# Two of three passes of a split-precision expert layer: weights instead of tokens held in TensorE for the second layers, sums kept transposed

## The chip, the cores and the metric

One NeuronCore of one Trainium2 chip. Times are device microseconds of one execution of the whole program.

## The reference

```
attn = softmax(mask(scale * q @ k^T)) @ v        # 4 x 8 heads, 576 tokens, window 32, half the heads dilated by 4
x    = attn as [2304 tokens, 512]
P    = exp(x @ w_gate - max); 8 rounds of row and column normalisation      # [2304, 8], the shares
for e in 0..7:  out += P[:, e] * (relu(x @ w1[e]) @ w2[e])                  # 512 -> 1024 -> 512
y    = activation(out @ w_in) @ w_out                                       # 512 -> 2048 -> 512, weights in float64
```

## The kernel before

The hidden dimension is cut into units of 512: two for each of the eight experts (16), and four for the last layer pair (called ffn in the code). The 2304 tokens are cut into three passes `k` of 768, each pass into two halves of 384 (`HALF`). Every product is made in split precision: an operand is kept as a high and a low float32r word, and `product` (L413) issues three matmuls for each 128-deep piece: high by high, high by low, low by high. The high word is a copy on ScalarE (L110), the low word a subtraction on VectorE (L111); in the text these are "highs" and "lows".

Unit 0 of all tokens is computed in six blocks of 384 tokens (`block_steps`), mixed by hand with the attention. The blocks of passes 1 and 2 (the last four) send their result to DRAM (`y_kept`). Then the list `runs` is worked off. Pass 0 is done unit by unit (units 1 to 15). Each of the passes 1 and 2 begins with unit 1 alone and goes on with seven pairs: both units of one expert. The ffn ends the program with two pairs for each pass.

A unit's `first_layer` makes 7 products of quarters (a Strassen scheme; `ORDER` is 1, 5, 6, 2, 7, 3, 4) of 12 matmuls each with 384 moving columns: 84 matmuls, in PSUM tiles `pa`, `pb`, `pc`, evacuated by ScalarE and VectorE into `kept`. Its `second_layer` holds 128 tokens in the array and streams 512 columns of the weights `w2o`: 6 token tiles by 4 pieces by 3, 72 matmuls into `py`, and VectorE adds each finished tile to the sum `acc` (tokens by model dimension), scaled by the token's share in `prob`, which is a per-partition scalar there.

A pair does two first layers (`F1`, `F2` below) and then `seven_second`: again 7 products of quarters, here of 256 columns of the weights: for each product 3 token tiles by 4 pieces by 3 matmuls, 252 in all, into `qh` or `qy`, `qt`, `qs` and `qx`. The operands for one product stand in one of three buffers `hh`, `hl`, `third`, written by highs and lows (class `Seven`) as the strings in `FIRST_WORK` and `SECOND_WORK` place them. A low is issued one product or more ahead of its use. After each token tile, VectorE's `join_scaled` (L578) adds the tile to `acc`, times its share.

After each pass `turn_steps` transposes `acc` on TensorE (24 transposes through `ident`, L1186), copies it to `xf` on ScalarE and sends it to `z_kept`, the ffn's input; then `y_kept` of the next pass is loaded into `acc`. All this lies within the first layer that follows.

Beside this runs `double_steps`: it converts the ffn's float64 weights on VectorE (L298 to L335), makes sums on GpSimd (L137, L264), splits and stores them. It is advanced a step at a time (`pull(double)`) at places counted in TensorE's order, in passes 1 and 2. All DMAs are issued by SP's queue, in program order. Engines run their own instructions strictly in order.

## Time and profile before

| | us |
|---|---|
| median of 3 runs | 1971.32 (1970.05 to 1971.91) |
| the profiled execution | 1969.49, of which the span 1967.7 |
| PE busy in the span | 1947.1 (99%) |
| DVE, ACT, POOL busy | 1475.8, 1011.0, 315.9 |
| granted TensorE clock | 1.00 of 2.4 GHz all through |

PE, DVE, ACT, POOL and SP are TensorE, VectorE, ScalarE, GpSimd and SyncE. The busy time of PE is the union of overlapping matmuls, so the time that a matmul costs is read from a stretch divided by its matmuls, not from the duration of one.

### The profile page before, as it was taken

How to read it: one execution, taken by the hardware profiler on the slowest of the kernel's cores; microseconds unless marked ns; L12 is line 12 of the kernel's file. 1: busy time of each engine (PE TensorE's matmuls, PEld its weight loads, DVE VectorE, ACT ScalarE, POOL GpSimd, SP SyncE). 2: the span in 40 equal slices, each digit the busy share in tenths (PEclk: the TensorE clock that was granted, in tenths of full speed). 3: DMA queues.
4: the chain of work that ended last, by engine and by line, in shares of the span. 5: the costliest groups of instructions: out<-in, count | busy, mean ns of one | idle time of the engine just before them, and what ended most of it. 6: DMA issues, size and time to landing. Idle time of an engine off the chain costs nothing.

```text
span 1967.7 us, 34404 instructions
## 1 busy us (share of the span) xinstructions
PE 1947.1 (99%) x12926; PEld 1864.6 (95%) x12926; DVE 1475.8 (75%) x2612; ACT 1011.0 (51%) x2179; POOL 315.9 (16%) x327
## 2 busy tenths in 40 slices
PE   8999999999999999999999999999999999999999
PEld 7888889899898989999999999999999999999999
DVE  6654698988888868686888668677987576876867
ACT  6655445455555445444445435443454355675555
POOL 4213133534544400001001000010011000000000
PEclk9999999999999999999999999999999999999999
DMA  7532577788787888898889977988898877787874
GB/s 167 125 73 85 199 270 278 300 313 311 290 326 299 333 339 305 296 325 324 294 317 328 320 269 279 344 287 314 296 330 320 286 248 283 257 293 269 288 242 145
DMA packets 222390, 539.41 MB, mean 274 GB/s; under 512 B 81040, under 2 KB 113296, under 8 KB 199824
## 3 DMA queue, kind: packets, MB, share of 16 engines
q1 hardware_dynamic: 222224, 537.21, 77.5%
q8 instruction: 102, 1.67, 0.3%
q14 instruction: 64, 0.52, 0.1%
HBM read 383.53 MB, written 153.62 MB: 273 GB/s over the span
## 4 chain that ended last, share of the span: by engine, by line
PE 93%; ACT 2%; DMA 2%; DVE 2%; issue 0%; POOL 0%; SPq 0%; ACTq 0%; POOLq 0%; DVEq 0%
PE pa L413 22%; PE py L413 17%; PE pc L413 11%; PE qy L413 9%; PE qh L413 9%; PE qt L413 9%; PE pb L413 5%; PE qs L413 3%; PE ph L413 3%; PE s L766 2%; PE qx L413 1%; DMA w_kept<-raw 1%; PE px L808 1%; PE pe L792 1%; PE pt L734 1%
## 5 line engine op out<-in xcount | busy, mean ns | idle before, releaser
L413 PE MATMUL pa<-xo,w1o 128*128 128x384 f32 x2736 | 513.7, 336 | 5.9 <-ACT kept L428 4.7
L413 PEld LDWEIGHTS pa<-xo,w1o 128*128 128x128 f32 x2736 | 476.1, 188 | 10.8 <-ACT kept L428 6.7
L413 PE MATMUL pc<-xo,w1o 128*128 128x384 f32 x1368 | 257.2, 335 | 0.8 <-DVE w1o L111 0.8
L137 POOL TENSOR_TENSOR raw<-raw 128x256 f32<-128x256 f32 x152 | 141.2, 957 | 704.5 <-DVE raw L325 170.7
L413 PE MATMUL py<-w2o,hh 128*128 128x512 f32 x816 | 251.5, 390 | 0.0
L413 PEld LDWEIGHTS pc<-xo,w1o 128*128 128x128 f32 x1368 | 238.5, 188 | 1.1 <-DVE w1o L111 1.1
L428 ACT ACTIVATE kept<-pa 128x384 f32<-128x384 f32 x228 | 110.0, 490 | 230.0 <-PE pa L413 228.1
L413 PEld LDWEIGHTS py<-w2o,hh 128*128 128x128 f32 x816 | 152.8, 188 | 30.2
L386 DVE TENSOR_TENSOR xf<-xf 128x768 f32<-128x768 f32 x180 | 167.3, 964 | 1.4
L413 PE MATMUL py<-w2o,hl 128*128 128x512 f32 x408 | 158.8, 389 | 0.0
L110 ACT ACTIVATE third<-xf 128x768 fp32r<-128x768 f32 (+1 forms) x124 | 95.2, 793 | 80.3 <-DVE xf L386 33.1
L111 DVE TENSOR_TENSOR w1o<-raw,w1o 128x256 fp32r<-128x256 f32 x210 | 125.0, 644 | 11.9 <-ACT w1o L110 11.9
L111 DVE TENSOR_TENSOR third<-xf,third 128x768 fp32r<-128x768 f32 (+1 forms) x124 | 115.5, 943 | 19.9 <-ACT third L110 17.9
L413 PE MATMUL pb<-xo,w1o 128*128 128x384 f32 x684 | 129.0, 335 | 0.0
L431 DVE TENSOR_TENSOR kept<-pb,kept 128x384 f32<-128x384 f32 x114 | 62.1, 554 | 84.6 <-PE pb L413 83.9
L1157 ACT ACTIVATE xf<-kept 128x384 f32<-128x384 f32 x168 | 86.2, 524 | 71.1 <-DVE kept L431 69.5
L413 PEld LDWEIGHTS pb<-xo,w1o 128*128 128x128 f32 x684 | 119.1, 188 | 0.0
L110 ACT ACTIVATE w1o<-raw 128x256 fp32r<-128x256 f32 x210 | 77.3, 414 | 70.1 <-POOL raw L137 70.1
L110 ACT ACTIVATE hh<-xf 128x768 fp32r<-128x768 f32 x92 | 74.7, 842 | 70.8 <-DVE xf L386 33.4
L110 ACT ACTIVATE hl<-xf 128x768 fp32r<-128x768 f32 x92 | 74.5, 842 | 63.1 <-DVE xf L386 25.8
L603 ACT ACTIVATE hh<-kept 128x384 fp32r<-128x384 f32 x102 | 53.7, 526 | 80.3 <-DVE kept L431 80.2
L111 DVE TENSOR_TENSOR hh<-xf,hh 128x768 fp32r<-128x768 f32 x92 | 86.8, 957 | 9.3 <-ACT hh L110 9.2
(191 smaller groups left out, 3543.7 us busy)
## 6 DMA issues: line engine op xcount, KB each, us to landing
w1o<-w_kept SPq DMA_DIRECT2D x294, 512.0 KB, 5.7
w2o<-w_sums SPq DMA_DIRECT2D x56, 1024.0 KB, 5.2
w_kept<-w1o SPq DMA_DIRECT2D x105, 512.0 KB, 4.2
w2o<-w_kept SPq DMA_DIRECT2D x40, 1024.0 KB, 5.3
w2x<-w_kept SPq DMA_DIRECT2D x24, 1024.0 KB, 5.7
w2x<-w_sums SPq DMA_DIRECT2D x24, 1024.0 KB, 5.6
w_kept<-w2o SPq DMA_DIRECT2D x23, 1024.0 KB, 6.4
w_kept<-raw SPq DMA_DIRECT2D x36, 512.0 KB, 7.2
```

Source lines behind the costliest of these rows:

```text
L110: nc.scalar.activation(out=hi, in_=raw, func=AF.Copy)
L111: return lambda: nc.vector.tensor_tensor(out=lo, in0=raw, in1=hi.bitcast(F32), op=ALU.subtract)
L137: nc.gpsimd.tensor_tensor(out=out[:, q], in0=in0[:, q], in1=in1[:, q], op=op)
L386: nc.vector.tensor_tensor(out=dst, in0=in0, in1=in1, op=ALU.subtract)
L413: nc.tensor.matmul(o, lhsT=a(h), rhs=b(l), start=first and n == 0, stop=last and n == 2, skip_group_check=on)
L428: nc.scalar.activation(out=dst, in_=src, func=AF.Copy)
L431: nc.vector.tensor_tensor(out=dst, in0=src, in1=dst, op=ALU.add)
L603: return [lambda: nc.scalar.activation(out=hi, in_=src, func=AF.Relu), lambda: nc.vector.scalar_tensor_tensor(out=lo, in0=src, scalar=0.0, ...
L734: nc.tensor.transpose(pt[:, pr, i * CH:(i + 1) * CH], raw[:, 2 * t + i, 2 * pr:2 * pr + 2, :].rearrange("p h e -> p (h e)"), ident[:CH, :CH])
L766: nc.tensor.matmul(s[:, i, :], lhsT=qd[:, pr, j, :], rhs=kt[:, pr, key0(j):key0(j) + KW], start=not early, stop=not early or i == JG - 1)
L792: nc.tensor.transpose(pt[:, i * P:(i + 1) * P], self.e[:, i, :], ident)
L1157: return [lambda: nc.scalar.activation(out=hid[:, half_, j, f], in_=src, func=AF.Relu)]
```

## The change

In passes 1 and 2 the sum `acc` is kept as model dimension by tokens (`acc_t`, the same tile read as 128 x 4 x 768). The second layers of unit 1, of the pairs and of the last four blocks of unit 0 now hold 128 x 128 of the weights in the array and stream 384 tokens. A token's share is now a column, so it can no longer be a per-partition scalar: `shares_steps` transposes `prob` once for each pass and stores it (`p_kept`), `load_shares` loads one expert's row, repeated over all partitions. A finished tile of a pair is multiplied by it on VectorE into a `kept` buffer (`scaled`) and added to `acc_t` on GpSimd. In unit 1, VectorE adds and GpSimd multiplies. `turn_steps` transposes only after pass 0; later it sends `acc_t` out as it is.

```diff
+    acc_t = acc.rearrange("p t d -> p (t d)").rearrange("p (c x) -> p c x", c=KC)
...
+    SECOND_TURNED = ([(f, c, 0) for f in (0, 2) for c in range(3)] + [(f, c, 1) for f in (1, 3) for c in range(3)]
+                     + [(f, c, 1) for f in (0, 2) for c in range(3)] + [(f, c, 0) for f in (1, 3) for c in range(3)]
+                     + [(f, 3, j) for j in range(2) for f in range(FC)])
+
+    def second_layer_turned(finish):
...
+            product(py[c, j], lambda h: w2o[:, h, f, c * P:(c + 1) * P],
+                    lambda h: hs[h][:, f, j * HALF:(j + 1) * HALF], left[c, j] == KC - 1, left[c, j] == 0)
+            if not left[c, j]:
+                finish(py[c, j], c, j)
+            yield "y"
...
+    def seven_second_turned(buf, tag):
...
+            for x in range(2):
+                o = chain[of][x]
+                for c in range(KC):
+                    product(o, lambda h: w[:, h, c, x * P:(x + 1) * P], lambda h: a[:, h, c, :],
+                            of == i and c == 0, c == KC - 1, of != i)
+                    if c == KC - 1:
+                        there = acc_t[:, d * 2 + x, j * HALF:(j + 1) * HALF]
+                        room = late.tile([P, HALF], F32, tag=f"kept{(2 - count) % 3}", bufs=2, name="scaled")
+                        count += 1
+                        nc.vector.tensor_tensor(out=room, in0=o, in1=at.shares[j], op=ALU.mult)
+                        nc.gpsimd.tensor_tensor(out=there, in0=room, in1=there, op=ALU.add)
+                    m = x * KC + c
+                    if m in (2, 5, 7):
+                        yield n, (2, 5, 7).index(m)
...
+        for f, c in [(f, c) for c0 in (0, 2) for f in range(FC) for c in (c0, c0 + 1)]:
...
+            product(py[c], lambda h: at.w2[f][:, h, cs], lambda h: hid[h][:, f, :HALF], f == 0, f == FC - 1)
+            if f == FC - 1:
+                here = at.stage()[:, :HALF]
+                nc.scalar.activation(out=here, in_=py[c], func=AF.Copy)
+                nc.sync.dma_start(out=y_kept[b // 2][:, c, b % 2 * HALF:(b % 2 + 1) * HALF], in_=here)
...
-    def join_scaled(e, k):
-
-        def join(o, i, x, d):
-            at_ = acc[:, x, d * HD:(d + 1) * HD]
-            nc.vector.scalar_tensor_tensor(out=at_, in0=o, scalar=prob[:, k * TPP + x, e:e + 1], in1=at_,
-                                           op0=ALU.mult, op1=ALU.add)
-        return join
+    def load_shares(e, k):
+
+        at.shares = [late.tile([P, HALF], F32, tag="r", bufs=2, name="shares") for _ in range(2)]
+        for j, x in enumerate(at.shares):
+            nc.sync.dma_start(out=x, in_=p_kept[k][e, j * HALF:(j + 1) * HALF].partition_broadcast(P))
+
+    def finish_turned(py, c, j):
+        o = acc_t[:, c, j * HALF:(j + 1) * HALF]
+        nc.vector.tensor_tensor(out=o, in0=py, in1=o, op=ALU.add)
+        nc.gpsimd.tensor_tensor(out=o, in0=o, in1=at.shares[j], op=ALU.mult)
...
-            share = {1: 33 / 48, 2: 60 / 48, 3: 26 / 48}
+            share = {1: 33 / 48, 2: 63 / 48, 3: 28 / 48}
...
+        def turn_steps(k, more):
+
+            if k:
+                yield
+                nc.sync.dma_start(out=z_kept[k].rearrange("p (c x) -> p c x", c=KC), in_=acc_t)
+                for _ in range(9):
+                    yield
+                if more:
+                    nc.sync.dma_start(out=acc_t, in_=y_kept[k + 1])
+            else:
...
-                    if m > 12 or u > 1 and m % 5:
+                    if m > 12 and (u > 1 or m % 3) or u > 1 and m % 5:
                         pull(double)
...
-                if e == 1 and m >= len(ORDER) * UQ - TPP:
-                    t = m - (len(ORDER) * UQ - TPP)
-                    nc.scalar.activation(out=acc[:, t, :], in_=acc[:, t, :], func=AF.Copy,
-                                         scale=prob[:, k * TPP + t, 0:1])
+                if moe and m == 4:
+                    load_shares(e, k)
...
-            for n_, t in seven_second((join_scaled if moe else join_plain)(e, k), bufs, tags[0]):
+            for n_, t in seven_second_turned(bufs, tags[0]) if moe else seven_second(join_plain(e, k), bufs, tags[0]):
```

Over the whole program TensorE has 3528 fewer matmuls of 256 columns (14 pairs by 252), 288 fewer of 512, 48 fewer transposes of 128, and 2736 more of 384 columns. VectorE has 294 fewer joins of 128x256 and 12 fewer of 128x512, and 212 more operations of 128x384 that read PSUM; GpSimd has 212 more of 128x384; SP issues 38 more DMAs.

TensorE, second layers of the first pair of pass 1, before; the right side names the operand streamed or held, a row is a whole product where its PSUM tiles have one name:

```order
L413 MATMUL qh<-w2x,third 128x256 x36
L413 MATMUL qt<-w2o,hh 128x256 x36
L413 MATMUL qh<-w2o,hl 128x256 x36
L413 MATMUL qs<-w2x,third 128x256 x24
L413 MATMUL qx<-w2x,third 128x256 x12
```

and at the same place in the changed kernel (line numbers there are its own):

```order
L415 MATMUL qy<-third,w2x 128x384 x24
L415 MATMUL qt<-hh,w2o 128x384 x24
L415 MATMUL qy<-hl,w2o 128x384 x24
L415 MATMUL qs<-third,w2x 128x384 x12
L415 MATMUL qx<-third,w2x 128x384 x12
```

The products stand in the same order and read the same buffers; each has 24 matmuls instead of 36.

VectorE at the start of the same second layers, before (`xf` are the sums for later products, `hl`, `third`, `hh` the lows):

```order
L386 TENSOR_TENSOR xf<-xf 128x768 x4
L578 SCALAR_TENSOR_TENSOR acc<-qh,prob,acc 128x256 x2
L111 TENSOR_TENSOR hl<-xf,hl 128x768
L578 SCALAR_TENSOR_TENSOR acc<-qh,prob,acc 128x256
L111 TENSOR_TENSOR hl<-xf,hl 128x768
L111 TENSOR_TENSOR third<-xf,third 128x768
```

and in the changed kernel:

```order
L388 TENSOR_TENSOR xf<-xf 128x768 x4
L573 TENSOR_TENSOR scaled<-qy,shares 128x384
L113 TENSOR_TENSOR hl<-xf,hl 128x768
L573 TENSOR_TENSOR scaled<-qy,shares 128x384
L113 TENSOR_TENSOR hl<-xf,hl 128x768
L113 TENSOR_TENSOR third<-xf,third 128x768
```

Two multiplications stand where three joins stood; the lows keep their places behind them.

GpSimd at the beginning of pass 1 in the changed kernel (L139 is the old L137; `raw` belongs to `double_steps`):

```order
L217 TENSOR_TENSOR xf<-xf 128x2x256 x8
L637 TENSOR_TENSOR acc<-acc,shares 128x384 x8
L574 TENSOR_TENSOR acc<-scaled,acc 128x384 x13
L139 TENSOR_TENSOR raw_7770<-raw_7770 128x2x128 x2
L574 TENSOR_TENSOR acc<-scaled,acc 128x384
L139 TENSOR_TENSOR raw_7770<-raw_7770 128x2x128 x6
```

Before, the eight `raw` sums stood there alone; now two of them stand ahead of a pair's last addition.

## Rows read from the trace of the kernel before

**Rows 1.** The page: busy time and share of each engine.
```profile
PE 1947.1 (99%) x12926; PEld 1864.6 (95%) x12926; DVE 1475.8 (75%) x2612; ACT 1011.0 (51%) x2179; POOL 315.9 (16%) x327
```

**Rows 2.** Stretches: us, busy time of each engine, clock, DMA share, GB/s.
```profile
0.00:248.96 248.96, 237.03 (x1877) 207.06 (x1877) 147.19 (x398) 143.85 (x507) 65.84 (x95) 1.00 0.48 132
248.96:1967.70 1718.74, 1710.11 (x11051) 1657.52 (x11050) 1328.64 (x2216) 867.15 (x1673) 250.07 (x232) 1.00 0.82 295
942.79:972.95 30.16, 30.16 (x253) 30.16 (x253) 27.57 (x48) 9.42 (x14) 2.35 (x3) 1.00 0.78 265
972.95:987.51 14.56, 14.56 (x86) 14.56 (x85) 10.04 (x20) 7.03 (x14) 0.97 (x1) 1.00 0.95 345
1151.05:1168.43 17.38, 17.38 (x110) 17.03 (x109) 11.69 (x20) 11.43 (x24) 0.00 (x0) 1.00 0.74 242
1604.40:1622.13 17.73, 17.56 (x110) 17.00 (x109) 11.19 (x18) 13.83 (x29) 0.00 (x0) 1.00 0.71 239
```

**Rows 3.** The chain that ended last: start us, us, what, how many.
```profile
528.53 16.32 PE py L413 x72
1002.41 4.31 PE qh L413 x36
1302.55 4.30 PE qh L413 x36
```

**Rows 4.** The second layers of all 14 pairs, columns as in rows 2: the fullest, the last line.
```profile
1276.52:1306.69 30.17, 30.17 (x254) 30.17 (x253) 28.30 (x50) 8.40 (x11) 1.62 (x2) 1.00 0.73 260
...
sum 422.32, PE 422.32 PEld 422.32 DVE 364.59 ACT 140.78 POOL 23.41; mean PE 30.17 PEld 30.17 DVE 26.04 ACT 10.06 POOL 1.67
```

**Rows 5.** GpSimd by line: count, ns min/median/max, first and last start, form.
```profile
L351 POOL TENSOR_TENSOR t<-xf,t x4: 1009/1015/1722, 190.2 to 215.6; 128x384 f32<-128x384 f32 x4
L264 POOL TENSOR_TENSOR raw<-raw x32: 727/744/2197, 933.5 to 1501.4; 128x256 f32<-128x256 f32 x32
```

**Rows 6.** VectorE by line, the same columns.
```profile
L431 DVE TENSOR_TENSOR kept<-pa,kept x114: 541/552/560, 246.2 to 1930.8; 128x384 f32<-128x384 f32 x114
L578 DVE SCALAR_TENSOR_TENSOR acc<-qh,prob,acc x84: 468/477/489, 766.3 to 1545.3; 128x256 f32<-128x256 f32 x84
L386 DVE TENSOR_TENSOR xf<-xf x180: 943/952/1501, 686.6 to 1953.9; 128x768 f32<-128x768 f32 x180
```

**Rows 7.** Timeline of three places: start us, us, engine, line, what [idle before].
```profile
994.20 2.36 DVE L386 TENSOR_TENSOR xf<-xf 128x768 f32<-128x768 f32 x2
994.43 2.73 POOL L264 TENSOR_TENSOR raw<-raw 128x256 f32<-128x256 f32 x2 [3.76 <-DVE raw L111]
...
1076.24 0.96 DVE L111 TENSOR_TENSOR hh<-xf,hh 128x768 fp32r<-128x768 f32 x1
1076.47 2.20 POOL L264 TENSOR_TENSOR raw<-raw 128x256 f32<-128x256 f32 x1 [32.46 <-DVE raw L111]
1077.11 0.96 DVE L386 TENSOR_TENSOR xf<-xf 128x768 f32<-128x768 f32 x1
1077.98 0.88 DVE L578 SCALAR_TENSOR_TENSOR acc<-qs,prob,acc 128x256 f32<-128x256 f32 x2
...
1297.85 1.49 DVE L111 TENSOR_TENSOR hh<-xf,hh 128x768 fp32r<-128x768 f32 x1
1300.38 0.94 DVE L111 TENSOR_TENSOR hh<-xf,hh 128x768 fp32r<-128x768 f32 x1
```

**Rows 8.** VectorE groups in 1276.52:1306.69: count, busy us, mean ns, idle before.
```profile
L578 DVE SCALAR_TENSOR_TENSOR acc<-qh,prob,acc 128x256 f32<-128x256 f32 x11 | 4.9, 477 | 1.4 <-PE qh L413 1.4
L578 DVE SCALAR_TENSOR_TENSOR acc<-qt,prob,acc 128x256 f32<-128x256 f32 x6 | 2.7, 478 | 0.4 <-PE qt L413 0.4
```

**Rows 9.** Timeline 1249 to 1256, the longest wait of TensorE after 250 us.
```profile
1254.74 0.42 ACT L110 ACTIVATE raw<-raw 128x256 fp32r<-128x256 f32 x1 [5.33 <-DMA w_kept<-raw]
1255.59 0.61 PE L413 MATMUL pa<-xo,w1o 128*128 128x384 f32 x2 [2.54 <-ACT kept L428]
```

**Rows 10.** DMA issues: what, count, KB each, median us to landing.
```profile
acc<-y_kept SPq DMA_DIRECT2D x2, 1536.0 KB, 13.2
```

More of the change, by code (lines that the diff above doesn't have):

```diff
@@ L551, in block_steps @@
             yield "act"
-        order = [(f, t) for f in range(FC) for t in range(2)] + [(f, 2) for f in range(FC)]
-        if b == NB - 1:
-            order = [(f, t) for f in range(FC) for t in range(TPH)]
         py = {}
-        for f, t in order:
-            if t not in py:
-                py[t] = bank("t" if t == 2 and b == NB - 1 else "y", 2, f"py{b}_{t}")
-            ts_ = slice(t * P, (t + 1) * P)
-            product(py[t], lambda h: hid[h][:, f, ts_], lambda h: at.w2[f][:, h], f == 0, f == FC - 1)
+        if b < 2:
+            for f, t in [(f, t) for f in range(FC) for t in range(2)] + [(f, 2) for f in range(FC)]:
+                if t not in py:
+                    py[t] = bank("y", 2, f"py{b}_{t}")
+                ts_ = slice(t * P, (t + 1) * P)
+                product(py[t], lambda h: hid[h][:, f, ts_], lambda h: at.w2[f][:, h], f == 0, f == FC - 1)
+                if f == FC - 1:
+                    nc.scalar.activation(out=acc[:, b * TPH + t, :], in_=py[t], func=AF.Copy)
+                yield "y"
+            return
+        for f, c in [(f, c) for c0 in (0, 2) for f in range(FC) for c in (c0, c0 + 1)]:
+            if c not in py:
+                py[c] = bank("t" if c > 1 and b == NB - 1 else "y", 2, f"py{b}_{c}")[:, :HALF]
+            cs = slice(c * P, (c + 1) * P)
+            product(py[c], lambda h: at.w2[f][:, h, cs], lambda h: hid[h][:, f, :HALF], f == 0, f == FC - 1)
             if f == FC - 1:
-                finish_first(py[t], b * TPH + t)
+                here = at.stage()[:, :HALF]
+                nc.scalar.activation(out=here, in_=py[c], func=AF.Copy)
+                nc.sync.dma_start(out=y_kept[b // 2][:, c, b % 2 * HALF:(b % 2 + 1) * HALF], in_=here)
             yield "y"
@@ L605, in act_relu @@
                                                        op0=ALU.max, op1=ALU.subtract)]
-    def finish_first(py, t):
-        k, x = divmod(t, TPP)
-        here = acc[:, x, :] if k == 0 else at.stage()
-        nc.scalar.activation(out=here, in_=py, func=AF.Copy)
-        if k:
-            nc.sync.dma_start(out=y_kept[k][:, x, :], in_=here)
     def finish_add(py, t):
@@ L1237, in tile_attention_moe_ffn @@
                 if kind_ == "moe":
-                    turn = turn_steps(k_, kind == "moe", "y" if kind == "moe" else tags[1])
+                    turn = turn_steps(k_, kind == "moe")
             prep2, ahead = ahead, iter(())
@@ L1245, in tile_attention_moe_ffn @@
                 finish = finish_add if u == 1 else finish_scaled(u)
+                if k:
+                    tags = ["y", "h"]
+                if u == 3:
+                    rows = shares_steps(late)
                 if ends:
@@ L1278, in tile_attention_moe_ffn @@
                         pull(turn)
+                    if u == 3 and m % 2:
+                        pull(rows)
                 drain(prep2)
```

59 lines of the change are left out of this document (45 added, 14 removed).

## The prediction

> **What bounds the kernel now.** I began with the page: TensorE is busy 99% of the span, VectorE 75%, ScalarE 51%, GpSimd 16% [rows 1]. A busy share can hide waits, so I cut the span into stretches [rows 2]. Up to 248.96 us (attention mixed with unit 0) TensorE is idle for 11.9 us; in the 1718.7 us after it, for 8.6 us. From there on the program lasts as long as TensorE's instructions take, and the question is what each of them costs.
>
> For that I divide stretches in which TensorE never stops by their matmuls. A pair's second layers are 252 matmuls of 256 columns in 30.16 us [rows 2]: 119.7 ns each (36 of them are 4.31 us in the chain [rows 3]). A first layer is 84 of 384 columns in 14.56 us [rows 2]: 173.3 ns. A unit's second layer is 72 of 512 columns in 16.32 us: 226.7 ns [rows 3]. From 256 to 384 columns it is 53.6 ns more, from 384 to 512 it is 53.4 ns more: 0.42 ns a column, and, drawn back to no columns, 12.5 ns that every matmul costs whatever its width. The granted clock is 1.00, its upper level of 2.4 GHz, in all of these stretches [rows 2].
>
> The Trainium skill ("TensorE: Matmul & The Clock Gate", Back-to-back issue gap) gives the isolated gap between matmuls as N/2.4 + 2.5 ns. By that figure, as an estimate, a pair's second layers would take 27.5 us before and 27.3 us after, and the 14 pairs would gain 3 us in all. The trace has 30.16 us for them [rows 2]; the measurement decides, and its fixed part is five times as large.
>
> **The change, part by part.**
>
> *Pairs.* Tokens streamed or weights streamed, the columns are the same (252 x 256 = 168 x 384), but there are 84 fewer matmuls. 168 x 173.3 ns = 29.12 us against 30.16: 1.04 us less for each pair, 14.6 us for 14.
>
> *Unit 1 in passes 1 and 2.* 72 x 226.7 = 16.32 us becomes 96 x 173.3 = 16.64 us: 0.6 us more for both. *The four blocks of unit 0:* 36 x 226.7 = 8.16 us becomes 48 x 173.3 = 8.32 us, 0.6 us more for all. Columns are the same again, matmuls are more.
>
> *The turns.* The first layer with the turn after pass 1 takes 17.38 us, the one after pass 2 17.73 us, against 14.56 us without one [rows 2]. With their 48 transposes, and the ScalarE copies that these wait for, 2.8 + 3.2 = 6.0 us go. Two small transposes of the shares come in: 2.8/24 = 0.12 us each by the same row, 0.2 us.
>
> TensorE's sum: -14.6 + 0.6 + 0.6 - 6.0 + 0.2 = -19.2 us, if nothing makes it wait.
>
> *The joins.* A pair loses 21 VectorE joins of 477 ns, which read PSUM, and gets 14 multiplications of 128x384 out of PSUM. The nearest row is L431, one PSUM and one SBUF input, 552 ns [rows 6]: 10.0 us against 7.7 us, 2.3 us less VectorE work. The 14 additions go to GpSimd: 128x384 took it 1.015 us in the median [rows 5], 14.2 us of a pair's 58 us, on an engine nearly idle there (1.67 us in the mean pair's second layers [rows 4]). Only later `scaled` and `kept` buffers wait for them: six go round, so an addition may be three products, 12 us, late. By themselves they cost nothing.
>
> *What the additions do to VectorE* is the uncertain term. GpSimd and VectorE seem to take turns where VectorE works from SBUF alone. At 1076.47 a sum of GpSimd that takes 0.744 us undisturbed [rows 5] lasts 2.20 us, until two such VectorE operations are through, and then runs beside the joins, which lose nothing. At 994.43 it gets in between: two of VectorE's 0.95 us operations take 2.36 us instead of 1.8. At 1297.85 a low takes 1.49 instead of 0.94 us [rows 7]. So a sum of 0.744 us costs VectorE 0.54 us or nothing; the 0.54 is 0.2 us less than it takes. Operations with a PSUM input never grow: L431 stays between 541 and 560 ns and the joins between 468 and 489, while L386, SBUF alone, reaches 1501 ns from 952 [rows 6]. An addition of 1.015 us then costs VectorE a price p between 0 and 0.8 us. Each stands right behind its multiplication, with a low next on VectorE (the order above), and behind the low about as often another multiplication, under which it fits for the most part, as another SBUF operation. If GpSimd always gets in, that is (0.3 + 0.8)/2 = 0.55 us; two of the three places above show it getting in. I take p = 0.45 us, with 0.35 to 0.55 for the forecast.
>
> The Trainium skill ("GPSIMD Engine Reference", section 1, Specifications) says that GpSimd shares its SBUF interfaces with VectorE, with contention for VectorE instructions that have two SBUF inputs or run in a 2-port mode. The trace agrees: 1.49 us beside 0.94 us for such a low [rows 7].
>
> Does it reach TensorE? In the fullest pair, at 1276.52, VectorE is busy 28.3 of 30.17 us [rows 4]. Its last low ends at 1301.32 [rows 7] and the product that needs it starts at 1302.55 [rows 3]: 1.2 us to spare. Up to that low some 10 additions will have run, 10p. Against it, 15 joins at 0.45 us, as they follow each other in [rows 8], less 10 multiplications at 0.52 are 1.5 us; 1.8 us in which VectorE waited for TensorE early on [rows 8] can be filled; TensorE comes 0.9 us sooner. So TensorE waits 10p - 1.5 - 1.8 + 0.9 - 1.2 = 10p - 3.6 us there, and in another pair less by what VectorE is less busy. Over the 14 pairs (five from 27.5 to 28.3 us, one at 27.0, the others below, with a mean of 26.0 for all 14 [rows 4]) this makes 0 us up to p = 0.35, 2.4 us at 0.45, 8 us at 0.55, 11 at 0.6 and 32 at 0.8. I take 2 us, and 0 and 11 as ends of the range.
>
> *Unit 1's sum.* `acc` of pass 2 is now loaded after `z_kept` has been sent from it: the load goes out some 2 us ahead of the second layer, takes some 13 us [rows 10], and the first of eight tiles is finished 16 x 3 x 173.3 ns = 8.3 us in. VectorE waits 3 us, but each tile has its own PSUM bank, so TensorE does not. What covers it are the banks: were they needed at once, it would be 3 us, once.
>
> *Loads of shares:* two for each pair, issued in its first layer and used two first layers later. SP stands there for the last additions, a microsecond or two; the weights queued behind it are for the next first layer, 10 us on. Nothing.
>
> *Stores.* TensorE's longest wait after 250 us, 2.54 us, is ScalarE standing at a high of `double_steps` whose buffer is still being stored (5.33 us), with an evacuation behind it [rows 9]. `double_steps` is advanced two steps more in each unit 1, so such meetings move a little: unchanged, 2 us either way. The mixed part before 249 us gets more `y` steps and shares to match: 0, 1.5 us either way.
>
> **Sum.** -19.2 + 2 = -17 us. Against the profiled execution (1969.49) that is 1952.5; that execution stands 1.8 us below the median of the three runs, and against the median, 1971.3, it is **1954.5 us**.
>
> **Rivals.**
>
> *A: no hindrance.* GpSimd waits as at 1076.47, p is under 0.35: 1971.3 - 19.2 = 1952, or 1950 with the stores' waits gone. Against: 994.43 and 1297.85 [rows 7].
>
> *B: much of the gain lost.* p between 0.55 and 0.65, waits of 8 to 15 us: 1960 to 1967. For it: GpSimd got in at two places of three. Against: half of the additions meet a multiplication.
>
> *C: slower.* VectorE becomes the bound of the pairs. It decides where the waits pass 19.2 us, at p = 0.68; at 0.8, each addition holding VectorE up for all of its time but 0.2 us, they are 32 us: 1984. For it: GpSimd was seen at 1.722 us once for 128x384 [rows 5], and a longer addition costs more. Against: the medians of 1.015 and 0.744 us [rows 5], and the multiplications, which it cannot hold up.
>
> *D: no change.* Two sums of `double_steps` stand ahead of a pair's last addition (the order above). Where such sums wait for a split that waits for a store, the addition waits, and so do ScalarE's copies into `kept`. Each place would cost like [rows 9], 2.5 us; with seven of them the gain is lost: 1971. Against: all waits after 249 us together are 8.6 us [rows 2].
>
> *E: the width is not what the pairs pay for.* If a pair stays at 30.16 us, only the turns are left: -6.0 + 1.4 = -4.6 us, 1966.7. Against: three widths lie on one line. A small fixed part per matmul, as in the gap rule that the Trainium skill gives ("TensorE: Matmul & The Clock Gate", Back-to-back issue gap), would come to nearly the same time, an estimated 1963.
>
> **How the numbers follow.** The forecast, 1952 to 1960, has 0.60; A 0.15; B 0.10; E 0.03; D 0.06; C 0.06. A measurement of this kernel tells 0.2%, 4 us, from no change. Forecast, A, B and E are faster: 0.88; same 0.06 (D); slower 0.06. The range goes from 1948 (A, less 2 us each for stores and the mixed part) to 1967, over B and E, and leaves out C and D.
>
> **What would show it.** Right: second layers of pairs at 29.1 us where VectorE has room, first layers after passes 1 and 2 at 14.6 us, multiplications at 552 ns, lows of 128x768 with a mean above 0.95 us in pairs, and TensorE's waits in pairs for L113 and nothing else, about 2 us in all. A: no such waits. B and C: such waits of over a microsecond in most pairs. D: ScalarE's copies into `kept` waiting for GpSimd. E: 180 ns a matmul in `qh` and `qy`. What would make the prediction wrong is above all a price of the additions to VectorE outside 0.35 to 0.55 us.

## The result, and the profile after

The changed kernel takes 1990.41 us in the median (1985.4 to 1992.08, 4 runs) against 1971.48 of the kernel before: ratio 1.0095, with an interval of 1.0079 to 1.0111. It is slower, by 19 us, where 17 us less was forecast. The profiled execution took 1992.08 us, with a span of 1990.1.

The page, as in [rows 1], and two of its costliest groups (columns: count, busy us, mean ns of one, idle time before them and what ended it):

```profile
PE 1947.3 (98%) x11800; PEld 1870.2 (94%) x11800; DVE 1547.7 (78%) x2520; ACT 1001.2 (50%) x2157; POOL 621.1 (31%) x539
...
L415 PE MATMUL pa<-xo,w1o 128*128 128x384 f32 x2736 | 517.4, 337 | 15.4 <-ACT kept L430 13.8
...
L574 POOL TENSOR_TENSOR acc<-scaled,acc 128x384 f32<-128x384 f32 x196 | 290.1, 1495 | 501.1 <-DVE scaled L573 501.0
```

TensorE has 1126 matmuls fewer and is busy for as long as before: a busy share does not tell that its clock fell in places, or that it waited. VectorE is busy 72 us longer, though the change was to take more work from it than it adds. An addition takes GpSimd 1.495 us in the mean, where [rows 5] gave 1.015.

The stretches, columns as in [rows 2]: up to unit 1's first second layer; the rest of pass 0; a pair's second layers without a wait; the first layers with the turns after passes 1 and 2.

```profile
0.00:257.15 257.15, 242.54 (x1924) 218.99 (x1925) 145.90 (x397) 144.79 (x511) 66.18 (x97) 0.95 0.47 129
257.15:727.15 470.00, 468.81 (x2377) 425.18 (x2377) 402.48 (x675) 245.29 (x544) 191.95 (x166) 1.00 0.81 301
892.88:922.13 29.25, 29.25 (x170) 29.25 (x169) 28.43 (x36) 11.12 (x18) 18.12 (x14) 1.00 0.80 272
1169.54:1184.10 14.56, 14.56 (x85) 14.56 (x85) 12.75 (x20) 7.57 (x15) 4.87 (x3) 1.00 0.96 310
1628.76:1643.33 14.57, 14.57 (x86) 14.57 (x86) 11.62 (x18) 9.38 (x18) 4.86 (x3) 1.00 0.92 337
```

Where nothing waits, the change does what its sum said: 29.25 us for a pair's second layers (29.12 forecast, 30.16 before), 14.56 and 14.57 us where the turns were. What went wrong is how often something waits, and the clock behind some of the waits. Sums over the 14 second layers of pairs (they answer to [rows 4]) and over the 29 first layers of passes 1 and 2 up to the last pair, these of the kernel after:

```profile
sum 423.66, PE 413.88 PEld 410.56 DVE 405.56 ACT 144.21 POOL 253.30; mean PE 29.56 PEld 29.33 DVE 28.97 ACT 10.30 POOL 18.09
...
sum 444.61, PE 431.59 PEld 426.45 DVE 322.64 ACT 244.20 POOL 93.32; mean PE 14.88 PEld 14.71 DVE 11.13 ACT 8.42 POOL 3.22
```

and the 29 first layers of the kernel before:

```profile
sum 432.00, PE 427.41 PEld 424.67 DVE 292.26 ACT 256.41 POOL 35.28; mean PE 14.74 PEld 14.64 DVE 10.08 ACT 8.84 POOL 1.22
```

Against the spans' difference of 22.4 us, the first part is 8.2 us longer (257.15 against 248.96), the second layers 1.3 us where 12.6 less were forecast, the first layers 12.6 us, though one of them lost a turn of 2.8 us; the rest, pass 0, unit 1 and the second turn, comes to nearly nothing. Of the 8.2 us, some 3.5 are not the change's: from 38.5 to 59.0 us TensorE's granted clock is 0.50 in this execution (hence the 0.95 in the first line), and in others of the same instructions it is not (below).

The two largest waits of TensorE from 257 us on (us in all, times, longest), and a third that lies in the pairs:

```profile
PE pa L415 <- ACT kept L430: 13.8, 13, 3.1
PE qh L415 <- DMA w2x<-w_kept: 5.3, 1, 5.3
PE qy L415 <- issue: 2.3, 3, 1.4
```

Ten of the thirteen waits for ScalarE lie in passes 1 and 2. Two of them in the timeline, as in [rows 9]:

```profile
987.61 3.27 POOL L266 TENSOR_TENSOR raw<-raw 128x256 f32<-128x256 f32 x4
990.23 0.63 ACT L112 ACTIVATE raw<-raw 128x512 fp32r<-128x512 f32 x1 [5.23 <-POOL raw L266]
990.76 0.47 ACT L430 ACTIVATE kept<-pa 128x384 f32<-128x384 f32 x1
991.29 0.69 PE L415 MATMUL pa<-xo,w1o 128*128 128x384 f32 x1 [2.72 <-ACT kept L430]
...
1067.77 0.63 ACT L112 ACTIVATE raw<-raw 128x512 fp32r<-128x512 f32 x1 [4.58 <-DMA w_kept<-raw]
1068.83 0.45 PE L415 MATMUL pa<-xo,w1o 128*128 128x384 f32 x1 [2.01 <-ACT kept L430]
```

ScalarE stands at a high of `double_steps` (the one until GpSimd's sums are through, the other until a store has left the buffer), and the copy into `kept` that frees TensorE's bank is the next in its queue. It is the wait of [rows 9], now many times. The wait for `w2x`, in the second layers that take 36.60 instead of 29.25 us, is a load that stands in SP's queue behind a store of `double_steps`, for whose low SP had waited 8.8 us:

```profile
1432.20 0.37 SPq L253 DMA_DIRECT2D w_sums<-raw  x1
1432.62 0.46 SPq L279 DMA_DIRECT2D xf<-in_moe_w_out_dram  x1
1433.20 0.75 SPq L203 DMA_DIRECT2D w2x<-w_kept  x1
...
1440.88 0.98 PE L415 MATMUL qh<-third,w2x 128*128 128x384 f32 x2 [5.32 <-DMA w2x<-w_kept]
```

Some of these waits cost more than themselves. The stretches right behind the three waits above (columns as in [rows 2]; the third number from the right is the granted clock, near 0.5, the lower level of 1.2 GHz, and in the second and fourth line 1.00 again):

```profile
991.20:994.60 3.40, 3.31 (x11) 3.31 (x12) 1.78 (x2) 2.19 (x6) 0.63 (x1) 0.56 0.99 390
994.60:996.00 1.40, 1.40 (x10) 1.40 (x9) 0.89 (x2) 0.40 (x1) 0.00 (x0) 1.00 0.98 248
1069.80:1073.00 3.20, 3.20 (x12) 3.20 (x12) 3.08 (x5) 1.98 (x6) 0.00 (x0) 0.54 1.04 419
1073.20:1075.00 1.80, 1.80 (x12) 1.80 (x11) 1.80 (x4) 1.53 (x3) 0.00 (x0) 1.00 0.28 114
1440.90:1444.90 4.00, 4.00 (x13) 4.00 (x14) 0.47 (x2) 0.00 (x0) 1.12 (x1) 0.52 1.00 382
```

Some 3.4 us at half the clock are 1.7 us lost. After 257 us the trace has four such stretches: behind the waits of 2.72 and 2.01 us and one of 3.14 us at 1515 us, 3.4 us each, and around the wait for `w2x`, 6.8 us. That is 17 us at the lower level, at most 8.5 us lost. The other waits are not followed by one.

In the first part, which both sides share but for the blocks' second layers, TensorE stands behind 192 us:

```profile
191.99 0.34 SPq L616 DMA_DIRECT2D y_kept<-big  x1
...
194.12 0.49 ACT L615 ACTIVATE raw<-py 128x384 f32<-128x384 f32 x1 [2.15 <-DMA y_kept<-big]
...
194.66 1.62 PE L415 MATMUL py<-xo,w1o 128*128 128x384 f32 x6 [1.84 <-ACT raw L615]
```

The first result of block 4 (the fourth of the six) is staged in the tile pool of the attention (`big`), the second in the pool that takes its place (`raw`), and the second was written only when the store out of the first had landed. The shares of the mixed part decide where that change of pools falls between the stores.

### The profile page after: what moved, and what is told of

Read it like the earlier page. It is cut to its first block, busy times and chain, and to the rows that moved or that the text cites. A ratio compares the mean times of both kernels' runs of the same rounds, so it can differ in the third digit from the quotient of the medians.

```text
span 1990.1 us, 32535 instructions
## 1 busy us (share of the span) xinstructions
PE 1947.3 (98%) x11800; PEld 1870.2 (94%) x11800; DVE 1547.7 (78%) x2520; ACT 1001.2 (50%) x2157; POOL 621.1 (31%) x539
## 4 chain that ended last, share of the span: by engine, by line
PE 73%; DVE 13%; DMA 6%; ACT 4%; issue 3%; POOL 1%; SPq 0%; ACTq 0%; DVEq 0%; POOLq 0%
PE pa L415 17%; PE py L415 14%; PE pc L415 8%; PE qh L415 6%; PE qy L415 6%; PE qt L415 5%; PE pb L415 4%; DMA w_kept<-raw 3%; PE ph L415 3%; DVE xf L388 2%; PE s L831 2%; PE pz L415 2%; DVE scaled L573 2%; PE qs L415 2%; DVE raw L113 1%
## 5 line engine op out<-in xcount | busy, mean ns | idle before, releaser
L574 POOL TENSOR_TENSOR acc<-scaled,acc 128x384 f32<-128x384 f32 x196 | 290.1, 1495 | 501.1 <-DVE scaled L573 501.0
L139 POOL TENSOR_TENSOR raw<-raw 128x256 f32<-128x256 f32 x152 | 142.9, 968 | 266.1 <-DMA raw<-in_moe_w_dram 114.0
L415 PE MATMUL py<-w2o,hh 128*128 128x512 f32 x720 | 222.0, 389 | 0.0
L388 DVE TENSOR_TENSOR xf<-xf 128x768 f32<-128x768 f32 x180 | 182.3, 1048 | 1.4
L415 PEld LDWEIGHTS py<-w2o,hh 128*128 128x128 f32 x720 | 134.8, 188 | 26.7
L113 DVE TENSOR_TENSOR third<-xf,third 128x768 fp32r<-128x768 f32 (+1 forms) x124 | 129.1, 1053 | 15.9 <-ACT third L112 15.8
L415 PE MATMUL py<-w2o,hl 128*128 128x512 f32 x360 | 140.0, 389 | 0.0
L113 DVE TENSOR_TENSOR w1o<-raw,w1o 128x256 fp32r<-128x256 f32 x210 | 122.3, 630 | 14.9 <-ACT w1o L112 14.8
L112 ACT ACTIVATE w1o<-raw 128x256 fp32r<-128x256 f32 x210 | 77.3, 414 | 68.5 <-POOL raw L139 67.2
L113 DVE TENSOR_TENSOR hl<-xf,hl 128x768 fp32r<-128x768 f32 x92 | 98.7, 1085 | 16.2 <-ACT hl L112 16.1
```

The lines of the kernel that those rows point to most:

```text
L112: nc.scalar.activation(out=hi, in_=raw, func=AF.Copy)
L113: return lambda: nc.vector.tensor_tensor(out=lo, in0=raw, in1=hi.bitcast(F32), op=ALU.subtract)
L139: nc.gpsimd.tensor_tensor(out=out[:, q], in0=in0[:, q], in1=in1[:, q], op=op)
L388: nc.vector.tensor_tensor(out=dst, in0=in0, in1=in1, op=ALU.subtract)
L415: nc.tensor.matmul(o, lhsT=a(h), rhs=b(l), start=first and n == 0, stop=last and n == 2, skip_group_check=on)
L574: nc.gpsimd.tensor_tensor(out=there, in0=room, in1=there, op=ALU.add)
```

## The experiments

Theory from the two traces: three separate losses. The additions hold VectorE up; `double_steps`, advanced 13 instead of 11 steps in each unit 1's second layer (its places are counted in TensorE's steps, and there are now more of them), stands elsewhere among ScalarE's work; the first block 4 stores straddle the change of pools. The rivals: that all of it is the additions, or the order of GpSimd's queue. The table holds all runs. Each ratio is to the kernel before run beside it, whose median there lay between 1969.45 and 1971.48 us, so medians of different rows compare to some 2 us. The last three columns are from the one profiled execution of each (start of unit 1's first second layer, sum of the 14 second layers, sum of the 29 first layers, us); without waits these sums would be 409.5 and 422.5 (14 times 29.25 and 29 times 14.57). The executions of one kernel lie further apart than many rows of the table (e8: 1969.9 to 1979.2 us, the profiled one being the longest).

| kernel | median us | ratio to before (95%) | begin | second | first |
|---|---|---|---|---|---|
| before | 1971.48 | 1 | 249.0 | 422.3 | 432.0 |
| after | 1990.41 | 1.0095 (1.0079 to 1.0111) | 257.2 | 423.7 | 444.6 |
| e1, no additions | 1972.21 | 1.0013 (0.9999 to 1.0026) | 253.7 | 413.1 | 439.3 |
| e2, additions on VectorE | 1985.47 | 1.0086 (1.0070 to 1.0103) | 253.0 | 418.5 | 446.1 |
| e3, sums on VectorE | 1992.13 | 1.0125 (1.0108 to 1.0141) | 255.1 | 423.4 | 447.8 |
| e4, copies for additions | 1969.95 | 1.0001 (0.9989 to 1.0013) | 252.3 | 414.5 | 435.4 |
| e5, steps as before | 1975.24 | 1.0026 (1.0013 to 1.0040) | 253.2 | 416.0 | 437.1 |
| e6, e5 and e2 | 1979.72 | 1.0041 (1.0023 to 1.0060) | 256.7 | 413.7 | 442.4 |
| e7, e5 and e1 | 1962.59 | 0.9959 (0.9944 to 0.9974) | 253.9 | 409.8 | 430.9 |
| e8, e6 and share | 1974.64 | 1.0018 (1.0003 to 1.0032) | 253.4 | 413.6 | 445.1 |
| e9, e5 and share | 1970.89 | 1.0011 (0.9999 to 1.0022) | 249.8 | 414.9 | 438.2 |
| e10, e9 spread | 1973.51 | 1.0020 (1.0005 to 1.0035) | 249.9 | 416.3 | 440.7 |
| e11, e8 spread | 1973.76 | 1.0013 (1.0000 to 1.0025) | 250.0 | 414.4 | 442.6 |
| e12, e7 and share | 1959.22 | 0.9959 (0.9947 to 0.9972) | 249.4 | 409.9 | 434.2 |
| e13, 8 additions, GpSimd | 1987.01 | 1.0090 (1.0073 to 1.0106) | 248.5 | 411.0 | 457.6 |
| e14, 8 additions, VectorE | 1992.69 | 1.0119 (1.0104 to 1.0134) | 249.4 | 411.3 | 459.3 |
| e15, e8, highs on GpSimd | 1971.45 | 1.0009 (0.9998 to 1.0021) | 249.5 | 415.9 | 436.3 |
| e16, e9, highs on GpSimd | 1982.11 | 1.0068 (1.0048 to 1.0087) | 249.6 | 421.6 | 443.2 |
| e17, before, highs on GpSimd | 1971.00 | 1.0002 (0.9991 to 1.0012) | 252.4 | 422.3 | 429.8 |
| e18, e15, lows later | 1973.59 | 1.0014 (1.0000 to 1.0028) | 251.8 | 414.9 | 441.5 |

**The additions (e1 to e4).**

```diff
# e1: the line goes; e2: on VectorE; e4: a copy with one input in its place (one of the two + lines each)
-                        nc.gpsimd.tensor_tensor(out=there, in0=room, in1=there, op=ALU.add)
+                        nc.vector.tensor_tensor(out=there, in0=room, in1=there, op=ALU.add)
+                        nc.gpsimd.tensor_copy(out=there, in_=room)
# e3: the sums of double_steps (the others, in prep_w1, likewise)
-                nc.gpsimd.tensor_tensor(out=out_, in0=in0, in1=in1, op=op)
+                nc.vector.tensor_tensor(out=out_, in0=in0, in1=in1, op=op)
```

e1: 

> The changed kernel without GpSimd's additions in the pairs (the multiplied tiles are thrown away, so the experts 1 to 7 are missing from the sums of passes 1 and 2). If the additions cause the waits, by hindering VectorE and by standing in GpSimd's queue: second layers of all pairs at 29.2 us, VectorE's 768-wide operations back at 0.95 us, time 1952 to 1960. If the waits come from the rest of the change (multiplications, loads of shares on SP's queue, steps of double_steps moved): waits in the pairs stay near 35 us and the time near 1988.

e2: 

> The changed kernel with the 14 additions of a pair on VectorE instead of GpSimd. VectorE gets 7.7 us more in a pair's second layers (about 31 us in a window of 29.2). If each addition costs VectorE some 0.5 us on GpSimd as well, and beside that holds up what stands behind it in GpSimd's queue, VectorE is no fuller than in the changed kernel and the queue is free: faster than the changed kernel, 1955 to 1975, with lows the only thing that TensorE waits for. If GpSimd's additions are innocent: slower than the changed kernel, over 1995.

e3: 

> The changed kernel with the sums of double_steps (64 of 128x256 in passes 1 and 2) on VectorE instead of GpSimd, additions still on GpSimd. If a good part of the waits comes from these sums standing behind additions in GpSimd's queue, with a high on ScalarE and evacuations behind it: the waits of first layers for kept go from some 16 us to under 6, time 1975 to 1982. If VectorE's lateness alone makes them: no better, 1986 to 1995, since VectorE gets 27 us more work.

e4: 

> The changed kernel with GpSimd's additions in the pairs replaced by copies of the multiplied tile (one SBUF input instead of two; the sums are then wrong). If GpSimd and VectorE get in each other's way through the two inputs of both: copies near 0.6 us that VectorE hardly feels, time 1955 to 1965. If any GpSimd work on SBUF hinders VectorE for as long as it lasts: in proportion to the time of a copy, 1968 to 1980.

Without the additions 18 us come back by the medians (16 by the ratios), but not the 36 that were missing: the second layers are nearly free of waits, the first layers still are 17 us above 422.5. By the time, neither expectation of e1 held. On VectorE the additions cost little less, which lies between the two expectations of e2; GpSimd's queue is free of them there, and the first layers are no shorter (446.1 us). The sums on VectorE change nothing for the better, though VectorE gets their work, so e3 alone does not clear GpSimd's queue; e2 and e3 together leave it little. Copies in the place of the additions cost nothing that can be told from e1. The time of e4 is that of its rival, and a copy took 0.987 us and not 0.6; but VectorE hardly felt it, as the theory had it, and what is left stands in the first layers. Two groups of VectorE in passes 1 and 2 (count, busy us, mean ns), first of the kernel after, then of e1, then of e4 with GpSimd's copies ahead:

```profile
L113 DVE TENSOR_TENSOR third<-xf,third 128x768 fp32r<-128x768 f32 x58 | 66.5, 1150 | 8.5 <-ACT third L112 8.5
L573 DVE TENSOR_TENSOR scaled<-qy,shares 128x384 f32<-128x384 f32 x56 | 30.6, 548 | 3.6 <-PE qy L415 3.4
```

```profile
L113 DVE TENSOR_TENSOR third<-xf,third 128x768 fp32r<-128x768 f32 x60 | 57.9, 970 | 8.3 <-ACT third L112 8.3
L573 DVE TENSOR_TENSOR scaled<-qy,shares 128x384 f32<-128x384 f32 x56 | 31.1, 555 | 20.7 <-PE qy L415 20.3
```

```profile
L574 POOL COPY acc<-scaled 128x384 f32<-128x384 f32 x173 | 170.4, 987 | 506.4 <-DVE scaled L573 506.4
...
L113 DVE TENSOR_TENSOR third<-xf,third 128x768 fp32r<-128x768 f32 x62 | 62.0, 1004 | 8.4 <-ACT third L112 8.4
```

The lows, from SBUF alone, grow with additions beside them (0.970 to 1.150 us) and hardly with copies (1.004); the multiplications, which read PSUM, do not (0.548 and 0.555). VectorE's busy time in the 14 second and 29 first layers is 405.56 + 322.64 us after and 345.65 + 287.03 in e1: 95.5 us for 196 additions, 0.49 us each. With copies it is 369.93 + 285.78, 0.12 us each.

**The place of double_steps, and the shares of the mixed part (e5 to e9, e12).**

```diff
# e5 and those built on it
-                    if m > 12 and (u > 1 or m % 3) or u > 1 and m % 5:
+                    if m > 12 and (u > 1 or m % 3 and m < 29) or u > 1 and m % 5:
                         pull(double)
# e8, e9, e12: besides, the share
-            share = {1: 33 / 48, 2: 63 / 48, 3: 28 / 48}
+            share = {1: 33 / 48, 2: 63 / 48, 3: 27 / 48}
```

e5: 

> The changed kernel with one condition more, so that double_steps takes 11 steps in each unit 1's second layer as before the change (after the change 13): its splits, stores and sums then stand among ScalarE's instructions in the pairs exactly where they stood before. The additions stay on GpSimd, the shares of the mixed part as changed. Theory (three separate losses: the additions beside VectorE, double_steps moved to where ScalarE stands with an evacuation behind it, the mixed part): the waits in first layers go, 11 to 16 us, also the 5.32 us for w2x; the waits for the additions in second layers stay: 1972 to 1980 us. Rival 1 (all of the loss is the additions; ScalarE's waits in first layers follow from VectorE being late): nothing changes, 1987 to 1992. Rival 2 (the moved steps are all of it): 1955 to 1962.

e6: 

> As the kernel with double_steps placed as before, and the 196 additions of the pairs on VectorE instead of GpSimd, so that GpSimd does what it did before the change and nothing runs beside VectorE from SBUF that did not run before. VectorE gets 14 additions of 128x384 more in each pair. Theory: the additions on VectorE delay TensorE in the fullest pairs by some us only (with double_steps moved this placing gave 1985.5, with second layers between 29.2 and 30.3 us but for one), and the waits in first layers go: 1958 to 1968 us. Rival 1 (the place of double_steps does not matter): 1983 to 1987, as before this edit. Rival 2 (VectorE is the bound of the pairs with these additions): second layers over 30 us in the full pairs, over 1970.

e7: 

> As the kernel with double_steps placed as before, and with the 196 additions of the pairs left out (so the pairs' outputs lack them; all else is computed). It tells what is left of the loss when the additions and the moved steps are both undone. Theory: only the mixed part's loss (3.5 to 5 us) and rows_steps (some 1.3 us) are left beside the predicted 1952 of a kernel in which nothing waits: 1955 to 1961 us. Rival 1 (double_steps' place does not matter): 1972, as without the additions alone. Rival 2 (the turns or the narrower matmuls give less than their stretches show): 1962 to 1970 with all second layers of pairs at 29.2 us.

e8: 

> As the kernel with the additions on VectorE and double_steps placed as before, and the share of the third block in the mixed part 27/48 instead of 28/48, so that the first stores of block 4 fall behind the change of tile pools instead of astride it. Theory: the wait of TensorE at about 192 us and the stretch at half the clock behind it, 3.5 to 5 us together, go: that much under the kernel without this edit run beside it, 1954 to 1964 us. Rival (the mixed part is longer because it holds more steps, wherever the stores fall): within 1 us of the kernel without this edit.

e9: 

> The changed kernel with two edits: double_steps placed as before (11 steps in each unit 1's second layer), and the third block's share 27/48 instead of 28/48, so that block 4's first stores fall behind the change of tile pools. The additions stay on GpSimd. Without the second edit it took 1975.2 us; the second edit alone was worth 5 us on the kernel with the additions on VectorE. Theory: the two losses are apart, so 1970 to 1972 us. Rival (the 5 us were chance of the clock's start): 1974 to 1976.

e12: 

> The changed kernel with all three suspected losses taken away: double_steps placed as before, the third block's share 27/48, and the 196 additions of the pairs left out (the pairs' outputs lack them). It took 1962.6 us with the share as changed. Theory (three losses are all there is): 1957 to 1959.5 us, near the predicted 1952.5 to 1954.5 of a kernel that hardly waits, less what rows_steps and ScalarE's last waits take. Rival (the share's 5 us do not come back here): 1961 to 1964.

One condition, which takes two steps of `double_steps` out of each unit 1, is worth 15 us (e5 against after; 13.6 by the ratios), and 10 us without additions (e7 against e1). By e5's profile 7.6 of its us are in the second layers, where the wait for `w2x` is gone, and 7.5 in the first. In these layers TensorE is idle for 22.8 us after and for 15.5 us in e5 (sums less PE's busy time), and where the trace of after has 17 us at half the clock behind 257 us, e5's has none: about half of the gain is waits, the rest mostly clock. The wait for `w2x` is in all five kernels with 13 steps (after, e1 to e4: 1.9 to 5.3 us) and in none with 11. That rules out that the additions are all. The theory put e6 too low: with the additions on VectorE the first layers still stand 20 us above 422.5, so the expected 1958 to 1968 was missed. 1979.7 is what its rival 2 said, over 1970 with the full pairs over 30 us (four are, 30.07 to 30.18), though the 14 together are only 4 us above 409.5. e7 is 1.6 us above the bound of its theory. The share is worth 5 us by the medians of e6 and e8, and 4 by those of e5 and e9; the start of unit 1 falls by 3.3 us each time, and with it the stand behind 192 us is gone. (The profiles of after, e6, e8 and e17 also have 20 us at half the clock at some 40 us, where others of the same order have none: e17 and before differ there by 3.4 us of their begin. What decides it is not shown, and the medians of kernels with few runs hold some of it.) Between e7 and e12 the begin falls by 4.5 us and the median by 3.4, but the ratio stays at 0.9959. TensorE is idle as long in both profiles' first layers (5.4 and 5.5 us); the 3.3 us that e12's are longer are two stretches of 3.4 us at half the clock. e9, the change with both places put right, cannot be told from the kernel before.

**Spreading double_steps (e10, e11).**

```diff
-                if not ends and m < 6:
+                if not ends and m < 4:
                     pull(double)
```

e10: 

> As the kernel with both of these edits, and 4 steps of double_steps instead of 6 in the first layer of a pair's second unit, so that it ends in the last pair of pass 2 but for one place instead of two pairs earlier: a little less VectorE and ScalarE work in each pair, and more time between its stores. Theory (ScalarE waits in the first layers because a high comes back to a buffer whose store takes some 9 us, two buffers going round): some of the waits in first layers go, 1963 to 1968 us. Rival (such meetings only move from place to place with any shift): within 3 us of the kernel without this edit, either way.

e11: 

> As the kernel with the steps spread over more of the two passes, but with the pairs' additions on VectorE. The kernel with the additions on VectorE and both other edits took 1974.6 us with waits of 20 us in its first layers. Theory: 1966 to 1971 us. Rival (meetings only move): 1972 to 1978. If the additions cost the same on either engine, it stands within 3 us of its sibling with them on GpSimd.

Nothing that can be told comes of less work in each pair: 2.6 us more and 0.9 us less, as the rival had it.

**Fewer additions (e13, e14).**

```diff
# e13, in place of the multiplication and the addition; parts holds the tiles of the first products
+                        if i in (1, 5, 6):
+                            parts[d, j, x] = room
+                            nc.scalar.activation(out=room, in_=o, func=AF.Copy)
+                        else:
+                            if i != 4:
+                                nc.vector.tensor_tensor(out=room, in0=o, in1=room, op=ALU.add)
+                            nc.vector.tensor_tensor(out=room, in0=o if i == 4 else room, in1=at.shares[j], op=ALU.mult)
+                            nc.gpsimd.tensor_tensor(out=there, in0=room, in1=there, op=ALU.add)
```

e13: 

> As the kernel with both edits (steps as before, third share 27/48), and in each pair the two products that go to one quarter of the output are summed before the share is multiplied: ScalarE copies the first product out of PSUM, VectorE adds the second to it and multiplies once, GpSimd adds the result to acc. A pair then has 8 additions on GpSimd instead of 14, VectorE 14 operations as before (6 of them from SBUF alone, 6 joins, 2 products), ScalarE 12 copies less 6, that is 6 more than before. By 6 x 0.49 us of hindrance less, VectorE is freed by about 3 us a pair. Theory (the 12 us are VectorE's time): about half of them come back, 1962 to 1967 us. Rival (ScalarE's meetings decide, and its copies wait for TensorE with splits behind them): 1970 us or more.

e14: 

> The same with the 8 additions on VectorE (0.56 us each) instead of GpSimd; with 14 additions there it took 1974.6 us. Theory: 3.4 us of VectorE work less in each pair, 1965 to 1970 us. Rival: 1973 us or more.

The theory fell. The second layers do what it said (411.0 us, 29.35 in the mean), but the first layers take 457.6 us, 19 more than in e9, and the kernel is 16 us slower. The waits of TensorE and ScalarE in e13 from 740 to 1610 us:

```profile
PE pa L415 <- ACT kept L430: 16.3, 10, 2.6
PE pa L415 <- DVE kept L433: 3.9, 4, 1.3
...
ACT raw L112 <- DMA w_kept<-raw: 43.5, 18, 5.9
ACT raw L112 <- POOL raw L266: 32.3, 3, 14.8
ACT scaled L577 <- PE qy L415: 24.6, 22, 1.6
```

ScalarE now also stands for TensorE at the six copies, in order, with highs behind. Of the 19 us, 12.4 are time in which TensorE is idle (22.5 against 10.1 us, sums less PE's busy time) and 5 the clock (four stretches of 3.4 us at half the clock against one). How the six copies bring the waits was not followed step by step.

**The highs of double_steps off ScalarE (e15 to e18).**

```diff
# in high(), only where double_steps calls it (a flag is cut here)
-        nc.scalar.activation(out=hi, in_=raw, func=AF.Copy)
+        nc.gpsimd.tensor_copy(out=hi, in_=raw)
# e18: besides, in parted()
             yield
+            yield
             low()
```

e15: 

> The changed kernel with the additions on VectorE, double_steps placed as before, the third share 27/48, and the highs of double_steps (fp32r copies of 128x512 and 128x256) on GpSimd instead of ScalarE. Without the last edit it took 1974.6 us, with some 20 us of waits in first layers. Theory (ScalarE stands at these highs, its copies into kept behind them): these waits go but for those of VectorE, 1958 to 1966 us. Rival 1 (VectorE stands at the lows behind the same highs, so it waits as long as ScalarE did and TensorE with it): 1972 to 1978. Rival 2: GpSimd's copies are slower than ScalarE's 0.63 us and everything of double_steps falls later: above 1978.

e16: 

> The same with the additions on GpSimd, where they now queue behind highs that wait for stores. Without the last edit it took 1970.9 us. Theory: the waits for ScalarE go, but some copies into kept wait for an addition that stands behind a high: 1962 to 1972 us. Rival (the additions' queue decides): above 1975.

e17: 

> The kernel before the change with these highs on GpSimd. It has 8.6 us of waits after 249 us in all, 2.5 of them behind such a high. Theory: 1966 to 1970 us, 0 to 4 us under the kernel before. Rival (VectorE now stands longer at the lows): 1971 to 1976.

e18: 

> As the kernel with the additions on VectorE and the highs of double_steps on GpSimd (1971.5 us), with one step more of double_steps between such a high and its low, so that VectorE reaches the low later and stands less. Theory (VectorE's stands at these lows keep the first layers waiting): 1964 to 1968 us. Rival (VectorE is full: its work itself is late, wherever the lows stand): 1969 to 1974.

In e15 the waits of TensorE for ScalarE's copies are gone from the list; those for VectorE have come in their place, and VectorE stands for the highs (735 to 1615 us, PE's rows, then VectorE's first):

```profile
PE pa L418 <- DVE kept L436: 4.6, 4, 2.7
PE pc L418 <- DVE kept L436: 1.9, 1, 1.9
...
DVE raw L116 <- POOL raw L113: 44.1, 23, 6.1
```

So ScalarE's standing was what the first layers waited for, and with it gone TensorE's idle time there falls from 12.8 us (e8) to 7.7. The time falls by 3 us (1971.45 against 1974.64, with intervals that overlap), not by the 9 to 17 expected: VectorE now stands at the lows behind the same highs. With the additions in the same queue (e16) it is 11 us worse than e9, as its rival had it. In the kernel before (e17) the edit changes nothing that can be told. One step more between high and low (e18) gives nothing either: the rival held.

No version that computes the whole beat the kernel before.

## Why the prediction was wrong

*Right.* The line through three widths: 168 matmuls took 29.25 us where 29.12 was forecast, in any second layer without a wait. With nothing in their way (e12) the 14 pairs take 409.9 us, 12.4 less than [rows 4], not 14.6, since 0.13 us a pair were missing from the sum and one still waits. The turns: 17.38 and 17.73 us became 14.56 and 14.57. Unit 1: 16.67 against 16.64; VectorE waited there 9.6 us for `acc` instead of 3, and TensorE, as forecast, not at all. The price p: 0.45 us taken, 0.49 (e1) and 0.46 (e12 against e9, worked out the same way) measured. But it was worked out from an addition of 1.015 us that costs all of its time less 0.2, and an addition took 1.495 in the mean (1.000 at the least): by that rule it would have cost more, so the agreement is in part luck.

*The step that failed first* is the one on stores: "`double_steps` is advanced two steps more in each unit 1, so such meetings move a little: unchanged, 2 us either way". It was worth 15 us (e5). The profile of before had three waits of TensorE for these copies in its 29 first layers, of 2.5 [rows 9], 1.6 and 0.2 us, and 8.6 us of waits in all [rows 2]; that was taken for what any order gives. It is what that one order gives: ScalarE stood at these highs 36 times before and 37 times after, and three waits of TensorE stood behind them before, eight of the ten after. They are also longer, 87 us in all before and 126 after: not for stores (68.5 and 55.8), but for VectorE's conversions (3.3 and 41.3) and GpSimd's sums (2.5 and 24.6). ScalarE's largest such waits from 740 to 1530 us (in all, times, longest), of the kernel before and then of the kernel after:

```profile
ACT raw L110 <- DMA w_kept<-raw: 47.6, 24, 5.4
ACT raw L110 <- DMA w_sums<-raw: 20.9, 8, 9.4
```

```profile
ACT raw L112 <- DMA w_kept<-raw: 42.1, 16, 4.6
ACT raw L112 <- DVE raw L337: 28.7, 6, 9.3
...
ACT raw L112 <- POOL raw L266: 24.6, 5, 9.1
...
ACT raw L112 <- DMA w_sums<-raw: 13.7, 5, 4.6
```

Every kernel of the changed form has more waits in its first layers, also those with ScalarE's old order, in which the same steps now meet other times (argued, not shown). And the sum had no term for the clock: up to 8.5 us behind 257 us in the profile of after, nothing in that of before.

*The step on the mixed part*, "0, 1.5 us either way", cost 3.3 to 4.5 us of the begin: with the shares 63/48 and 28/48 block 4's first stores fall astride the change of pools. The time of steps was counted there, and not which buffers they meet.

*The additions' term*, +2 us from 10p - 3.6, was mis-sized. e9 against e12 gives 5.0 us in the second layers, and 4.0 in the first layers, for which the sum had nothing: GpSimd's additions run on into the first layers, the same 0.46 us fall on VectorE's lows and sums there too (327.77 against 291.12 us busy), and it has the joins of `kept` to do. In the medians e9 and e12 lie 11.7 us apart. In the pairs the wait was not the one of the sum, either: in the profiles of after and e9 no wait there is for a low (L113). The waits that the trace lists as "issue" end 0.1 us after a multiplication out of a bank of the same name, so what TensorE waits for there seems to be the bank that a late VectorE has not yet freed. The longest:

```profile
1502.10 0.55 DVE L573 TENSOR_TENSOR scaled<-qy,shares 128x384 f32<-128x384 f32 x1
...
1502.74 0.93 PE L415 MATMUL qy<-hh,w2o 128*128 128x384 f32 x4 [1.45 <-issue]
```

*Smaller.* `shares_steps` (`rows_steps` in the expectations) took 1.2 us and not 0.2: the first layer of unit 3 is 15.83 us in e9 against 14.59 before, 0.8 of it a wait of the transpose for VectorE's copy.

*The rivals.* C had the sign and nearly the time, 1984, but not the mechanism: p is 0.46 to 0.49, not 0.8. D, the sums of `double_steps` ahead of the additions, came close in kind, ScalarE's copies into `kept` being late. Of the ten such waits, six follow a high that waited for a store, one a high that waited for GpSimd's sums, and one a copy that waited for an addition; with these sums off GpSimd (e3), or the additions (e2), little or nothing came back. A and B fell with p; E with the 29.25 us.

*Left open.* e12 stands at 1959.2, 5 us above the 1954.5 forecast for a kernel that also had the additions, with its first layers 11.6 us above 422.5. Why the kernels with eight additions wait so much longer in the first layers (e13, e14) is not shown. A third buffer for the stores, which would test them directly (6.9 us to landing in the median for the 36 of 512 KB to `w_kept`), was not tried. The edits were taken out in one order, and their sizes depend on it: the steps are worth 15 us with the additions and 10 without.

## What to carry to other kernels

Where a program of steps is woven into another by counting, a change of the counts moves every meeting of the two: compare the order of the engine that stands (here ScalarE) before and after, and put the old one back before measuring the change itself. A tuned order's few waits are no measure of what another order will have. Work given to an idle engine can have a price on a busy one, in all stages in which it runs: look for it in the durations of the busy engine's instructions (here 0.46 to 0.49 us for each addition, 0.12 for each copy).

## What was not expected of the hardware

The waits of TensorE of 2.01, 2.72 and 5.32 us shown above go with 3.4 us or more at a granted clock of 0.5; the wait of 2.54 us in [rows 9] does not, nor does one of 2.71 us in e15, while one of 1.27 us in e12 does. GpSimd's copies of 128x384 (one input) cost VectorE 0.12 us each, its additions (two inputs) 0.46 to 0.49, though a copy, 0.987 us, is as long as two thirds of an addition.
